# A spectral filter followed by an MLP: eight one-batch units in fixed order, per-row 64-point matrices, a single-pass 49-point stage back, and batch 0's first corner turn on TensorE

## Chip, cores and metric

One core of one Trainium2 chip. The metric is device time in microseconds (us) of one execution. Medians are over the runs of one kernel on one chip; every later kernel was timed together with the kernel before on the same chip (runs 9 to 11 on another chip than runs 1 to 8 and 12, so across these the ratios are what to compare). One of the first three runs of the kernel before took 1411.37 us; it is an outlier.

TensorE is PE in the profile, its weight loads PEld, VectorE DVE, ScalarE ACT, GpSimd POOL, SyncE SP. A suffix q (ACTq, SPq) marks a row in which the engine's sequencer issues something, such as a DMA.

## The reference

```python
X = np.fft.rfft(x, axis=1)                     # x: 8 x 3136 x 256, f32
y = np.fft.irfft(X * (filt_r + 1j * filt_i)[None], n=3136, axis=1)
xt = y.transpose(0, 2, 1)
h = xt @ U @ V                                 # U: 3136 x 32, V: 32 x 3136
u = y + h.transpose(0, 2, 1)
out = u + np.maximum(u @ w_ch1, 0.0) @ w_ch2   # w_ch1: 256 x 1024, w_ch2: 1024 x 256
```

Both kernels factor 3136 as 64 x 49. A batch goes through a 64-point stage, a corner turn through DRAM (store in one layout, load in another: the tiles `asb` out, `a2` in), a 49-point stage, the filter product, a 49-point stage back, a second corner turn (`esb` out, `e2` in), and a last 64-point stage that also adds the low-rank term. Then comes the MLP: eight steps of two hidden-layer matmuls per group of 512 tokens, with the second layer of the group before woven in.

## The kernel before

Five units of 1, 1, 2, 2 and 2 batches. Each middle is a generator; a plan deals its pieces over the MLP steps of earlier units. The parts that matter here:

```python
UNITS = [[0], [1], [2, 3], [4, 5], [6, 7]]
# ... first 64-point stage f1: one matrix wx for all rows, evicted to asb, stored to ct1
pf = ps.tile([128, 2, 512], F32, tag="w", bufs=1, name="pf")
nc.tensor.matmul(pf[:, i, :], wx, u.x[c][:, r:r + 2, :], start=True, stop=True)
# ... the middle: 49-point stage, products with both halves of the filter,
nc.vector.tensor_mul(uv.rearrange("p (f b d) -> p f b d", f=2, b=nb), zin, fin)
# ... and the 49-point stage back: two accumulating passes
for l in range(2):
    nc.tensor.matmul(pe[0:98, 0:bd], g3[:, (2 * k + l) * 98:(2 * k + l + 1) * 98],
                     uv[:, l * bd:(l + 1) * bd], start=(l == 0), stop=(l == 1))
# ... the low-rank term: the spectrum is loaded from DRAM once more, in another layout (eh)
nc.sync.dma_start(eh[c][2 * a:2 * z], dram(u.ct2, ...))
nc.tensor.matmul(ph[32 * g:32 * g + 32, 0:bd], ut2[:, rp * RANK:(rp + 1) * RANK], eh[c][:, i, :],
                 start=(rp < 4), stop=(rp >= 20 and g != 0))
```

Of the kernel before, what the change touches and what calls it, by code (L numbers as in the profile page):

```python
# [12 lines left out]
RELU = mybir.ActivationFunctionType.Relu  # L13

# [5 lines left out]
UNITS = [[0], [1], [2, 3], [4, 5], [6, 7]]  # L20


def _consts():
    f16 = np.float16
    w64 = np.exp(-2j * np.pi * np.outer(np.arange(NQ), np.arange(NQ)) / NQ)
    w49 = np.exp(-2j * np.pi * np.outer(np.arange(NR), np.arange(NR)) / NR)
    tw = np.exp(-2j * np.pi * np.outer(np.arange(NQ), np.arange(NR)) / SEQ)


    wf1 = np.zeros((NQ, 64))  # L30
    wf1[:, 0:31] = w64.real[:, 1:32]
    wf1[:, 31] = w64.real[:, 0]
    wf1[:, 32:63] = w64.imag[:, 1:32]
    wf1[:, 63] = w64.real[:, 32]



    perm = np.arange(NR)
    perm[25:] = 73 - perm[25:]
    tf2 = np.zeros((NK, 98, 98))  # L40
    for a in range(31):
        wp = (w49 * tw[a + 1][None, :])[perm, :]
        tf2[a, 0::2] = np.concatenate([wp.real.T, wp.imag.T], axis=1)
        tf2[a, 1::2] = np.concatenate([-wp.imag.T, wp.real.T], axis=1)
    tf2[:, :, NR + 25:98] *= -1.0
    w0, w32 = w49 * tw[0][None, :], w49 * tw[32][None, :]
    tf2[31, 0::2, 0:25] = w0.real.T[:, 0:25]
    tf2[31, 0::2, NR + 1:NR + 25] = w0.imag.T[:, 1:25]
    tf2[31, 1::2, 25:NR] = w32.real.T[:, 0:24]
    tf2[31, 1::2, NR + 25:98] = w32.imag.T[:, 0:24]  # L50
    tf2[31, 1::2, NR] = w32.real.T[:, 24]
    tf2 = np.concatenate([tf2, tf2[:, :, 0:NR]], axis=2)

    ctw = np.exp(2j * np.pi * np.outer(np.arange(33), np.arange(NR)) / SEQ)
    g = np.zeros((NK, 2, 98, 98))
    for a in range(31):
        t1 = (w49.conj() * ctw[a + 1][:, None]) / SEQ
        tr, ti = t1.real.T[perm, :], t1.imag.T[perm, :]
        g1, g2 = g[a, 0], g[a, 1]
        g1[:NR, :NR], g1[:NR, NR:] = tr, ti  # L60
        g1[NR:, :NR], g1[NR:, NR:] = -tr, -ti
        g2[:NR, :NR], g2[:NR, NR:] = -ti, tr
        g2[NR:, :NR], g2[NR:, NR:] = -ti, tr
        g2[25:NR, :] *= -1.0
        g2[NR + 25:98, :] *= -1.0
    t0 = (w49.conj() * ctw[0][:, None] / SEQ).T
    t32 = (w49.conj() * ctw[32][:, None] / SEQ).T
    g1, g2 = g[31, 0], g[31, 1]
    g1[0, :NR] = t0.real[0]
    g1[NR, NR:] = t32.real[24]  # L70
    g1[1:25, :NR], g1[NR + 1:NR + 25, :NR] = 2 * t0.real[1:25], -2 * t0.real[1:25]
    g2[1:25, :NR], g2[NR + 1:NR + 25, :NR] = -2 * t0.imag[1:25], -2 * t0.imag[1:25]
    g1[25:NR, NR:], g1[NR + 25:98, NR:] = 2 * t32.real[0:24], -2 * t32.real[0:24]
    g2[25:NR, NR:], g2[NR + 25:98, NR:] = -2 * t32.imag[0:24], -2 * t32.imag[0:24]

    w = np.exp(2j * np.pi * np.outer(np.arange(NQ), np.arange(33)) / NQ)
    s2 = np.zeros((64, NQ))
    s2[0:62:2] = 2.0 * w.real[:, 1:32].T
    s2[1:62:2] = -2.0 * w.imag[:, 1:32].T
    s2[62] = w.real[:, 0]  # L80
    s2[63] = w.real[:, 32]

    wf1d = np.zeros((128, 320))
    s2t = np.zeros((64, 320))
    for h in range(2):
        wf1d[h::2, 64 * h:64 * h + 64] = wf1
        wf1d[h::2, 128 + h:256:2] = wf1
        s2t[:, 128 * h + h:128 * h + 128:2] = s2.T
    wf1d[0:64, 256:320] = wf1
    s2t[:, 256:320] = s2.T  # L90

    kr = np.zeros((128, 96))
    for i in range(4):
        kr[32 * i:32 * i + 32, 64:96] = np.eye(32)
    return (wf1d.astype(f16),
            tf2.transpose(1, 0, 2).reshape(98, NK * 147).astype(f16),
            g.transpose(2, 0, 1, 3).reshape(98, NK * 2 * 98).astype(f16),
            s2.astype(f16),
            s2t.astype(f16),
            kr.astype(f16))  # L100


class Unit:
    def __init__(self, n, batches):
        self.n = n
        self.b = batches
        self.nb = len(batches)
        self.bd = self.nb * DM
        self.gt = self.nb
        self.ng = 6 * self.nb  # L110
        self.nr = 8 // self.nb
        self.x = {}
        self.e2 = {}
        self.ready = False
        self.h1 = None
# [3 lines left out]
def kernel(  # L119
# [12 lines left out]
    wf1_np, tf2_np, g_np, s2_np, s2t_np, kr_np = _consts()  # L132

    def inline(a, name):
        return nc.inline_tensor(np.ascontiguousarray(a), name=name).ap()

    wf1_d, tf2_d, g_d = inline(wf1_np, "wf1"), inline(tf2_np, "tf2"), inline(g_np, "g3")
    s2_d, s2t_d, kr_d = inline(s2_np, "s2"), inline(s2t_np, "s2t"), inline(kr_np, "kr")

    units = [Unit(n, b) for n, b in enumerate(UNITS)]  # L140
    for u in units:
        u.ct1 = nc.dram_tensor(f"ct1_{u.n}", (NR, 64, u.bd), F16, kind="Internal")
        u.ct2 = nc.dram_tensor(f"ct2_{u.n}", (32, 98, u.bd), F16, kind="Internal")
# [3 lines left out]
    ps = ctx.enter_context(tc.tile_pool(name="ps", bufs=2, space=bass.MemoryType.PSUM))  # L147
# [3 lines left out]



    def load_x(u, c, after=None):
        st = SEQ * DM if u.nb == 2 else 24 * DM
        if c == 3 * u.nb:
            t = sb.tile([128, DM], F16, tag="xl", bufs=2, name="xl")
            if after is not None:
                hold(t[0:1, 0:1], after)
            src = [[NR * DM, 64], [st, u.nb], [1, DM]] if u.nb == 2 else [[NR * DM, 64], [1, DM]]  # L160
            nc.gpsimd.dma_start(t[0:64 * u.nb],
                                dram(x.tensor, (u.b[0] * SEQ + 48) * DM, src))
        else:
            t = sb.tile([128, 8 * DM], F16, tag="x", bufs=4, name="x")
            if after is not None:
                hold(t[0:1, 0:1], after)
            nc.gpsimd.dma_start(t, dram(x.tensor, (u.b[0] * SEQ + 8 * c) * DM,  # L167
                                        [[NR * DM, 64], [st, 2], [1, 8 * DM]]))
            t = t.rearrange("p (r d) -> p r d", d=DM)
        u.x[c] = t  # L170

    def hold(dst, src):

        nc.vector.tensor_copy(dst, src)

    wf1 = cst.tile([128, 320], F16)
    nc.sync.dma_start(wf1, wf1_d)
    for c in range(4):
        load_x(units[0], c)
    tf2 = cst.tile([98, NK * 147], F16)  # L180
    s2 = cst.tile([64, 64], F16)
    kr = cst.tile([128, 96], F16)
    s2t = cst.tile([64, 320], F16)
    g3 = cst.tile([98, NK * 2 * 98], F16)


    fab = cst.tile([98, 2, NK, DM], F16)

    def load_filters(a, z):

        n = min(z, 31) - a
        for p0, src in ((0, filt_r), (NR, filt_i)):
            nc.gpsimd.dma_start(
                fab[p0:p0 + 25, 0, a:a + n, :],
                dram(src.tensor, (a + 1) * DM, [[64 * DM, 25], [DM, n], [1, DM]]))
            nc.gpsimd.dma_start(
                fab[p0 + 25:p0 + NR, 0, a:a + n, :],
                dram(src.tensor, (63 - a) * DM, [[64 * DM, 24], [-DM, n], [1, DM]]))
        if z == NK:
            for p0, src in ((0, filt_r), (NR, filt_i)):  # L200
                nc.gpsimd.dma_start(fab[p0 + 25:p0 + NR, 0, 31, :],
                                    dram(src.tensor, 32 * DM, [[64 * DM, 24], [1, DM]]))
            nc.gpsimd.dma_start(fab[0:25, 0, 31, :], dram(filt_r.tensor, 0, [[64 * DM, 25], [1, DM]]))
            nc.gpsimd.dma_start(fab[NR + 1:NR + 25, 0, 31, :],
                                dram(filt_i.tensor, 64 * DM, [[64 * DM, 24], [1, DM]]))
            nc.gpsimd.dma_start(fab[NR:NR + 1, 0, 31, :],
                                dram(filt_r.tensor, 1568 * DM, [[DM, 1], [1, DM]]))

    def mirror_filters(a, z):
        nc.sync.dma_start(fab[0:NR, 1, a:z, :], fab[NR:98, 0, a:z, :])  # L210
        nc.sync.dma_start(fab[NR:98, 1, a:z, :], fab[0:NR, 0, a:z, :])

    PARTS = [0, 8, 16, 24, NK]
    KA = PARTS[1] * 98
    load_filters(PARTS[0], PARTS[1])
    usb = sb.tile([64, NR * RANK], F16, tag="och", bufs=2, name="usb")
    vnat = sb.tile([128, SEQ], F16, tag="och", bufs=2, name="vnat")
    w1sb = cst.tile([128, 2 * 1024], F16)
# [7 lines left out]
    def second_loads(src):  # L226
        for i in range(2, 4):
            load_part(i, src)
# [499 lines left out]
```

## Time and profile before

| | before |
|---|---|
| time, median | 632.64 us (630.98 to 1411.37, 3 runs); 630 to 632 in later sets |
| span of the profiled run | 629.3 us, mean granted clock 0.926 |
| busy: PE / DVE / ACT / POOL | 552.8 / 330.0 / 334.6 / 41.7 us |
| DMA | 110.18 MB |

Busy time of PE is not the price of its work, because matmuls overlap in the trace: one of 512 columns is recorded as 0.38 us long, and in a full stretch the next starts 0.22 us after it. The price is the distance from one start to the next, and the prediction works with that. The strip below is from the page of the kernel before. The span is cut in 40 slices of 15.7 us; a digit is the busy share in tenths.

```profile
PE   3294576999699993989999999999999999999997
```

From slice 19 on PE is full, but for the end. Before it, PE is short of data in places.

### The profile page before, as it was taken

Reading aid. Unit: us, or ns where it says so; the run is one execution under the profiler, and the core shown is the slowest. Engines: PE = TensorE matmul, PEld = TensorE weight load, DVE = VectorE, ACT = ScalarE, POOL = GpSimd, SP = SyncE. Lnnn points to the kernel's source line nnn. Section 1 sums busy time; section 2 is a strip of 40 time slices with the busy share of each in tenths; the row PEclk is TensorE's granted clock in tenths of the full one; section 3 lists DMA queues with packets and bytes.
Section 4 is the critical chain, followed back from the end, with each engine's and each line's share of the span. In section 5 each row is a group of like instructions: output and inputs, shape, how many; then the busy total and the mean of one; then the engine's idle time right before and its main releaser. Section 6 shows DMA issues by size and latency. Waiting matters only on the chain.

```text
span 629.3 us, 10769 instructions
## 1 busy us (share of the span) xinstructions
PE 552.8 (88%) x4350; PEld 388.0 (62%) x4350; DVE 330.0 (52%) x390; ACT 334.6 (53%) x623; POOL 41.7 (7%) x62
## 2 busy tenths in 40 slices
PE   3294576999699993989999999999999999999997
PEld 0183242767456661657766676777677767777776
DVE  5274222786278870263888743576866325333332
ACT  0043232667156662546667665665766655666663
POOL 3345110100000000000000000000000000000000
PEclk9558576999979997989999999999999999999999
DMA  9898979999835749868567787455433862331112
GB/s 176 230 205 193 214 183 236 246 250 244 244 119 161 216 81 286 208 166 227 171 187 173 208 245 249 156 148 187 120 131 119 239 202 83 99 100 67 66 67 102
DMA packets 68002, 110.18 MB, mean 175 GB/s; under 512 B 5549, under 2 KB 49438, under 8 KB 66604
## 3 DMA queue, kind: packets, MB, share of 16 engines
q1 hardware_dynamic: 36240, 81.17, 41.2%
q0 software_dynamic: 7312, 15.91, 15.8%
q10 hardware_dynamic: 24400, 12.41, 6.9%
q8 instruction: 34, 0.56, 0.4%
q14 instruction: 16, 0.13, 0.1%
HBM read 72.38 MB, written 51.38 MB: 197 GB/s over the span
## 4 chain that ended last, share of the span: by engine, by line
PE 73%; DMA 16%; issue 4%; DVE 3%; ACT 2%; ACTq 1%; POOL 0%; SPq 0%; POOLq 0%; DVEq 0%
PE phh L550 25%; PE pc L590 24%; PE pe L360 8%; PE pz L382 5%; PE pu L532 3%; PE pc L564 3%; DMA x<-in_x_dram 3%; PE pf L304 3%; DMA ct_3<-asb 2%; DMA g_78<-g 2%; DMA eh<-ct_1 2%; ACTq L320 1%; DMA eh<-ct_2 1%; DMA ct_0<-asb 1%; PE ph L476 1%
## 5 line engine op out<-in xcount | busy, mean ns | idle before, releaser
L550 PE MATMUL phh<-ut,w1sb 128*128 128x512 f16 (+2 forms) x848 | 251.7, 377 | 3.5 <-DVE ut L539 3.0
L397 DVE TENSOR_TENSOR uv<-pz,fab 98x1024 f16<-98x1024 f32 (+1 forms) x128 | 137.8, 1087 | 35.3 <-PE pz L382 34.8
L600 DVE COPY och<-pc 128x512 f32<-128x512 f32 x96 | 66.3, 690 | 165.8 <-PE pc L564 162.6
L550 PEld LDWEIGHTS <-w1sb 128*128 128x128 f16 x848 | 105.6, 146 | 36.7 <-issue 16.7
L366 ACT CAST esb<-pe 98x512 f16<-98x512 f32 (+1 forms) x160 | 79.5, 501 | 64.6 <-PE pe L360 57.0
L360 PE MATMUL pe<-uv,g_78 98*98 98x512 f16 (+1 forms) x320 | 85.7, 353 | 1.4 <-DMA g_78<-g 0.8
L539 DVE CAST ut<-pu 128x1024 f16<-128x1024 f32 (+1 forms) x51 | 59.9, 1174 | 21.6 <-PE pu L532 21.4
L564 PE MATMUL pc<-idn,ut 128*128 128x128 f16 x394 | 54.8, 220 | 0.0
L360 PEld LDWEIGHTS <-g_78 98*98 98x98 f16 x320 | 41.3, 132 | 19.4 <-issue 5.6
L564 PEld LDWEIGHTS <-ut 128*128 128x128 f16 x394 | 38.7, 98 | 6.7 <-issue 0.3
L382 PEld LDWEIGHTS <-tf_74 98*98 98x98 f16 x160 | 21.7, 136 | 20.2 <-DMA a_163<-ct_0 15.3
L304 PE MATMUL pf<-x,wf_64 128*128 128x512 f16 x84 | 27.9, 402 | 6.8 <-DVE ut L539 6.3
L476 PE MATMUL ph<-eh,ut_94 128*32 128x512 f16 (+1 forms) x120 | 10.7, 384 | 26.2 <-DMA eh<-ct_0 11.6
L167 POOL DMA_DIRECT2D x<-in_x_dram x24 | 14.1, 602 | 266.5 <-PE pf L304 225.1
L309 DVE CAST asb<-pf 128x1024 f16<-128x1024 f32 x21 | 25.6, 1219 | 11.5 <-PE pf L304 8.9
L307 ACT CAST asb<-pf 128x1024 f16<-128x1024 f32 x21 | 21.3, 1013 | 10.7 <-PE pf L304 6.7
L390 DVE TENSOR_TENSOR uv<-pz,fab 98x512 f16<-98x512 f32 x32 | 20.9, 687 | 5.1 <-PE pz L387 2.9
L476 PEld LDWEIGHTS <-ut_94 128*32 128x32 f16 x120 | 3.3, 97 | 31.6 <-issue 20.7
L366 ACT ACT_TABLE_LOAD x1 | 1.3, 1283 | 30.2 <-DVE uv L390 30.2
L382 PE MATMUL pz<-a_161,tf_74 98*98 98x256 f16 x8 | 3.2, 403 | 15.2 <-DMA a_163<-ct_0 14.9
L532 PEld LDWEIGHTS <-eb_97 96*128 96x128 f16 x256 | 10.3, 100 | 7.5 <-issue 4.7
L486 ACT CAST hp<-ph 128x512 f16<-128x512 f32 (+1 forms) x5 | 2.5, 501 | 23.1 <-PE ph L483 23.1
(1427 smaller groups left out, 1046.2 us busy)
## 6 DMA issues: line engine op xcount, KB each, us to landing
out_dram<-och SPq DMA_DIRECT2D x48, 512.0 KB
x<-in_x_dram POOLq DMA_DIRECT2D x24, 512.0 KB, 8.0
ct_2<-esb SPq DMA_DIRECT2D x16, 196.0 KB
ct_3<-esb SPq DMA_DIRECT2D x16, 196.0 KB
ct_4<-esb SPq DMA_DIRECT2D x16, 196.0 KB
ct_2<-asb ACTq DMA_DIRECT2D x6, 512.0 KB
ct_3<-asb ACTq DMA_DIRECT2D x6, 512.0 KB
eh<-ct_2 SPq DMA_DIRECT2D x6, 512.0 KB
```

The costliest lines, as they stand in the source:

```text
L304: nc.tensor.matmul(pf[:, i, :], wx, u.x[c][:, r:r + 2, :], start=True, stop=True)
L309: nc.vector.tensor_copy(dst, pf)
L360: nc.tensor.matmul(pe[0:98, 0:bd], g3[:, (2 * k + l) * 98:(2 * k + l + 1) * 98], uv[:, l * bd:(l + 1) * bd], start=(l == 0), stop=(l == 1))
L366: nc.scalar.copy(st["esb"][:, i, :], pe[0:98, 0:bd])
L382: nc.tensor.matmul(pz[0:98, 0:bd], wz, a2[c][:, i, :], start=True, stop=True)
L397: nc.vector.tensor_mul(uv.rearrange("p (f b d) -> p f b d", f=2, b=nb), zin, fin)
L532: nc.tensor.matmul(pu[:, dh, 64 * i:64 * i + 64], e2[0:96, d0:d0 + 128], sv[0:96, 64 * r:64 * r + 64], start=(i == 0), stop=True, skip_gro ...
L539: nc.vector.tensor_copy(gr.ut[:, :, 0:n].rearrange("p h (c q s) -> p h c q s", q=64, s=2), pu[:, :, 0:n].rearrange("p h (c s q) -> p h c q ...
L550: nc.tensor.matmul(ph[:, 0:n], w1v[:, dh, :, t], gr.ut[:, dh, 0:n], start=(dh == 0), stop=(dh == 1))
L564: nc.tensor.matmul(o[:, dh * 128:dh * 128 + 128], gr.ut[:, dh, t0:t0 + n], idn, start=False, stop=(dh == 1), skip_group_check=True)
L590: nc.tensor.matmul(o, gr.h[tt][:, i * 128:(i + 1) * 128], w2sb[:, tt * DM:(tt + 1) * DM], start=(tt == 0), stop=False, skip_group_check=True)
L600: nc.vector.tensor_copy(dst, gr.pc.rearrange("p (j d) -> p j d", j=2))
```

## The change

The intent: give TensorE less work (one pass instead of two in the 49-point stage back; no reload of the spectrum for the low-rank term), and give the scheduler nothing to decide, with one fixed program order of eight equal units, so that the losses of the first half go away. The diff is 1247 lines; its core:

```diff
-UNITS = [[0], [1], [2, 3], [4, 5], [6, 7]]
+NB = 8
+    ctx.enter_context(tc.manual_schedule())
 ...  # 64-point stage: one matrix per row, twiddle inside
-    nc.tensor.matmul(pf[:, i, :], wx, u.x[c][:, r:r + 2, :], start=True, stop=True)
+    nc.tensor.matmul(pf[:, i * DM:(i + 1) * DM], wf[:, 8 * c + 2 * j + i, :], xt[b, c][:, 2 * j + i, :], ...)
 ...  # its result is stored by ACT, as before, from two buffers (three before)
+    asb = sb.tile([128, 8, DM], F16, tag="asb", bufs=2, name="asb")
+    nc.scalar.dma_start(dram(ct1[b], ...), asb[64 * h:64 * h + 64])
 ...  # batch 0: x is the weight, so the result comes out turned; copied to fc, then transposed
+    nc.tensor.matmul(z[:, 128 * i:128 * i + 128], xt[0, c][:, g + i, 128 * hh:128 * hh + 128],
+                     wf[:, 8 * c + g + i, :], ...)
+    dst = free(fc, 0, 128, 3136 * hh + 2 * (24 * h + 8 * c + g), [[2, 4], [1, 2], [98, 32]])
+    src = z.rearrange("p (i h c a) -> p h i c a", h=2, c=2, a=32)[:, h]
+    nc.vector.tensor_copy(dst, src)          # or nc.scalar.copy
 ...  # low rank in the spectrum: U is transformed once (uh), esb is read where it lies
+    nc.gpsimd.tensor_add(uh[:, :, p:p + 8], t[0], t[1])
+    nc.tensor.matmul(ph[32 * g:32 * g + 32, 0:DM], uh[:, a, :], esb[b, a // 4][:, a % 4, :], ...)
 ...  # the complex product: three products on DVE, one sum on POOL, then one pass on PE
+    nc.vector.tensor_mul(ta, pz, va)
+    nc.vector.scalar_tensor_tensor(out=tb[0:64], in0=pz[64:128], scalar=-1.0, in1=vb, op0=MULT, op1=MULT)
+    nc.vector.tensor_mul(tb[64:128], pz[0:64], vb)
+    nc.gpsimd.tensor_add(ys[k], ta, tb)
 ...
+    nc.tensor.matmul(pe[0:98], g3[:, m, :], v, start=(n == 0), stop=(n == len(parts) - 1))
 ...  # order of the start
+    u_hat()
+    for c in range(4):
+        turned(c)
+    mid_first()
+    ...                                      # load_e2, low_rank(0), put_h
+    stage4(groups[0], 0)
+    stage4(groups[0], 1)
+    for _ in st1(1):
+        pass
```

Batch 0 keeps the two passes. All of batch 0's transform and batch 1's first stage now stand ahead of the first hidden-layer matmul; the moment at which that matmul starts is called T0 below.

## The prediction

> **What bounds the kernel now.** I read three views, in this order: the busy table by stretches of time (length, then busy time and instruction count of PE, weight load, DVE, ACT, POOL, then granted clock, DMA share, GB/s), the PE timeline inside the last stretch, and the chain that ended last (start, length, what it was).
>
> ```profile
> 0.00:120.00 120.00, 69.66 (x394) 44.80 (x395) 49.02 (x89) 33.87 (x71) 34.22 (x49) 0.72 0.91 207
> 120.00:300.00 180.00, 158.54 (x1202) 106.84 (x1201) 105.04 (x120) 97.37 (x192) 6.33 (x11) 0.93 0.76 202
> 300.00:620.00 320.00, 319.79 (x2708) 232.07 (x2706) 174.16 (x180) 201.69 (x356) 1.15 (x2) 1.00 0.48 149
> ```
>
> From 300 us on TensorE has no idle time and the full clock; before that it is badly fed.
>
> ```profile
> 560.07 0.63 PE L532 MATMUL pu<-sv,eb_97 96*128 96x64 f16 x16
> 560.54 0.28 PE L590 MATMUL pc<-w2sb,h_6564 128*128 128x256 f16 x1
> 560.65 0.27 PE L590 MATMUL pc<-w2sb,h_6574 128*128 128x256 f16 x1
> ...
> 561.85 0.28 PE L564 MATMUL pc<-idn,ut 128*128 128x128 f16 x2
> 561.96 0.60 PE L550 MATMUL phh<-ut,w1sb 128*128 128x512 f16 x2
> 562.40 0.27 PE L590 MATMUL pc<-w2sb,h_6564 128*128 128x256 f16 x1
> ...
> 261.63 0.40 PE L476 MATMUL ph<-eh,ut_94 128*32 128x512 f16 x4
> 261.96 0.28 PE L590 MATMUL pc<-w2sb,h_2636 128*128 128x256 f16 x1
> ```
>
> Start to start is the real price of a matmul: 0.217 us for 512 columns (0.44 for two), 0.109 for 256, 0.055 for 128, 0.029 for 64 (0.47/16). Four low-rank matmuls with 32 weight columns start within 0.33 us, 0.083 each. Pricing every matmul of the kernel before: hidden layer, second layer, residual and last DFT stage of the 48 full groups 378 us; small groups 8.6; first DFT stage 21.3; the 49-point stage forward 31.3 and back 55.5 (192 x 0.217 + 128 x 0.109); low rank and its 96-row merge 9.4; rest 0.7. Sum 505 us. The matmuls in 300:620 price at about 316 us, so there the prices hold to 1.5%. That leaves 184 us of work in the first 300 us: **116 us are lost there**, and 5 at the end.
>
> ```profile
> 9.72 7.16 DMA ct_0<-asb
> 16.96 6.25 DMA ct_0<-al
> 23.25 4.47 DMA a_161<-ct_0
> 28.58 10.14 DMA g_78<-g
> ...
> 69.42 13.53 DMA x<-in_x_dram
> ...
> 159.70 9.85 DMA eh<-ct_1
> ...
> 230.67 10.60 DMA ct_3<-asb
> 241.27 7.31 DMA eh<-ct_2
> ```
>
> The losses are round trips through DRAM and loads on the path: batch 0's first corner turn (9.7 to 27.7), the tables (28.6), batch 1's x while the MLP already runs (69.4), and the low-rank reload of the spectrum (eh) at 159.7 and 241.3.
>
> **What the Trainium skill says.** (1) "TensorE: Matmul & The Clock Gate", Back-to-back issue gap: N/2.4 + 2.5 ns when warm, 216 ns at 512. The trace agrees (0.43 to 0.44 us for two). (2) The same page, Part 3 on packing: matmuls with few output rows placed in different column groups run together. It agrees, 0.33 us for four. (3) "VectorE: DVE Perf Modes", the perf-mode tier table: tensor_tensor with a PSUM operand runs at 1x. It agrees: 687 ns at 512 elements and 1221 at 1024 is 1.04 ns per element. So a product over 64 partitions should cost what one over 128 does. (4) "GPSIMD Engine Reference", section 3.1: about 2.6 cycles an element for a two-input op, so an estimate of 2.2 us for the new 1024-element adds; no run here shows it yet.
>
> **The change part by part.**
>
> *49-point stage back.* It was two accumulating passes per element; now it is one for batches 1 to 7, because the complex filter product is summed on DVE and POOL first. Batch 0 keeps two. Matmuls: 135 x 0.217 + 18 x 0.109 = 31.2 us instead of 55.5: **-24 us of PE**. Forward stays at 31.2.
>
> *Low rank in the spectrum.* It reads the esb tiles from SBUF, so the reload of eh goes (27 loads, about 12.8 MB) with its waits. 256 x 256 columns: I scale 0.083 by half, 256 x 0.042 = 10.7, plus 0.9: +2 us of PE.
>
> *First stage.* One 64-point matrix per row, so 168 x 256 columns instead of 84 x 512, same columns: 19 us, and 2.8 for batch 0. Transposes for batch 0: 64 x 0.055 = +3.5.
>
> PE sum after: 378 + 8 + 22 + 31 + 31 + 12 + 3.5 + 1 = **486 us against 505**. Only 19 us come from less work; the rest has to come from the 116 us.
>
> *Prologue.* Program order is fixed now, and all of batch 0 and the first stage of batch 1 precede the first MLP matmul. I work out that moment, T0. Loads: 6.2 MB by the software queue; its whole traffic is 15.9 MB at 15.8% of 629 us, or 160 GB/s, so 39 us; some 3.8 MB by hardware queues at about 310 GB/s, 12 us; data is there by about 52 us. Compute: two DVE memsets of 4096 words (4.3 us each, from 0.27 us at 256 words), the 3136-element copy (3.3) and eight products (3.2) end near 16 us; the turned first stage ends near 21; then ACT is the limit of batch 0's middle: 8 copies of 1024 (1.0) + 5 of 1024 (1.0) + 16 of 512 (0.586) = 22.4 us, to about 46. Storing and reloading the second corner turn takes 8 to 9 (store 2.5, load 3, h rows 2.5), to 55; st1(1), 13 evictions and 7 stores issued from ACT, 8 more. **T0 = about 64 us**, close to the loads, with 21 us of priced work done. In the kernel before, the MLP starts at 74 us but only runs freely from 114 and stops again at 160 and 230.
>
> *After T0.* 486 - 21 = 465 us of PE, at the 1.5% of the steady stretch 472. Batch 1's second corner turn has only 5 steps between its stores and its first use while x of batch 2 loads: 8 us. Other stalls: below, 8. End after the last matmul: 5.4 as now. Span 64 + 472 + 8 + 8 + 5 = 557; the time on record is 3.3 us over the span, so **561 us**.
>
> **Do the other engines keep up?** In a middle phase a step (one eighth of a group) costs PE 0.98 for the MLP + 4 x 0.217/4.3 + 0.06 = 1.24 us. DVE: three products of 1.22 per 4.3 steps (0.85) + output copies 0.17 + ut 0.09 = 1.11. ACT: 0.60 + esb 0.27 + asb 0.16 + ut 0.08 = 1.11, plus DMA issues. Both near 89%, against 54 and 63% in the kernel before's last stretch. POOL: 2.2 per 4.3 steps.
>
> **The rivals.** (a) *DVE or ACT becomes the bound in the middle phases.* For: 89%, strict order, one pz pair of banks, one eviction bank. Against: the plan leaves about four steps between the last product and its use, and averages over a batch are 82% (ACT) and 71% (DVE). If half-partition products cost 1.6 us or the POOL add slows DVE, seven phases of 34 steps lose 0.1 to 0.2 us a step, 25 to 45 us: 585 to 605. (b) *The prologue is bound by DMA or the order of waits.* For: DMA share 0.91 in the first 120 us, and ACT-issued stores took 4.1 and 5.2 us per pair at 93.7 and 98.9. Then T0 is 80 or more: 575 to 580. (c) *All waits vanish*: T0 58 and no stalls: 538. (d) *The gain is only the PE work*, because the losses move to other transfers: 632 - 19 = 613. Against: the biggest named waits (eh reloads, g table, batch 0's corner turn) have no counterpart in the new code.
>
> **Range and chances.** Low end (c); high end (a) and a part of (b): 540 to 597. Faster by over 2% needs under 620; even (d) gives that. Faster 0.95, same 0.04, slower 0.01.
>
> **What would show each step.** Right: total PE matmul work falls though the count rises; first hidden-layer matmul between 58 and 72 us; PE over 95% busy from about 80 us on, clock 1.0; ACT between 380 and 420 us busy in all, DVE near 340; POOL adds 2.0 to 2.6 us; no wait on a reload before the low-rank matmuls. Wrong: PE gaps every few steps on pz or y (rival a), T0 past 80 (rival b), stage-back matmuls waiting for POOL, or gaps at unit borders waiting for e2 loads (rival d).

## The result

| | before | after |
|---|---|---|
| time, median | 632.92 us (4 runs) | 624.1 us (621.3 to 626.36, 4 runs) |
| span profiled | 629.3 us | 621.1 us |
| busy PE / DVE / ACT / POOL | 552.8 / 330.0 / 334.6 / 41.7 | 514.4 / 360.9 / 397.6 / 174.0 us |
| matmuls | 4350 | 4467 |
| DMA | 110.18 MB | 95.31 MB |

The ratio is 0.9877, with a 95% interval of 0.983 to 0.9925. Ratios and intervals here are from fast runs timed together, so not quite the ratio of the medians quoted. Executions over 1.5% slower than the fastest of the same kernel are left out of the means. The kernel is 1.2% faster, and 63 us slower than predicted. PE's busy time fell by 38 us, yet the span fell by 8.

The strips of the kernel after (slices of 15.5 us):

```profile
PE   2128545898899889999999889998989889999997
DMA  9971485369656584696548775697364454443212
```

The start is worse fed than before: PE is below 0.6 in slices 1 to 7 but for slice 4, and DMA is not full for much of that time either (slices 3 to 5 and 7). And the long full stretch of the kernel before has become a row of nines and eights: a little is lost everywhere. In the busy table by stretches, cut at T0 (length, then busy time and count of PE, PEld, DVE, ACT, POOL, then clock, DMA share, GB/s):

```profile
0.00:98.00 98.00, 37.95 (x288) 25.77 (x289) 48.40 (x46) 41.62 (x52) 44.54 (x53) 0.89 0.67 137
98.00:621.00 523.00, 476.49 (x4179) 350.48 (x4178) 312.45 (x327) 355.93 (x668) 129.45 (x76) 0.99 0.58 157
```

Against the prediction's price of PE's work, 505 us before and 486 after, the losses are 629.3 - 505 = 124 us before and 621.1 - 486 = 135 us after. So PE's work fell by 19 us and the losses rose by 11: **the waits that the prediction named (the reload of `eh`, the tables, batch 0's first corner turn) did go, and losses of the same size came.** After, 98 - 21 = 77 us are lost ahead of T0 and 523 - 465 = 58 after it.

Not all of this loss is waiting. PE stood idle for 629.3 - 552.8 = 76.5 us before and for 621.1 - 514.4 = 106.7 after; the other 48 and 28 us lie inside its busy time, where it ran slower than the price. The kernel before was busy for 6.73 of the 7 us from 73 to 80, at a granted clock of 0.58. So the idle time grew by 30 us and the slow running shrank by 19, while the mean clock rose from 0.926 to 0.972.

**Ahead of T0.** The timeline of the kernel after at the start, VectorE first (start, length, what; in brackets the idle time before it and what ended it):

```profile
13.28 2.01 DVE L229 TENSOR_TENSOR ut<-psum,tw 98x256 f32<-98x256 f32 x4 [0.96 <-PE psum L224]
28.43 2.00 DVE L229 TENSOR_TENSOR ut<-psum,tw 98x256 f32<-98x256 f32 x4 [13.14 <-POOL uh L233]
30.28 14.74 DVE L294 CAST fc<-psum 128x256 f16<-128x256 f32 x12
```

DVE did half of its eight products by 15.3 us and then stood for 13.14 us, because it needed the buffers that POOL's sum `uh` (L233) reads. The same kernel on GpSimd:

```profile
27.07 0.57 POOL L210 DMA_DIRECT2D w2sb<-in_moe_w_ch_dram  x1
27.63 1.44 POOL L233 TENSOR_TENSOR uh<-ut 98x256 f16<-98x256 f32 x2
```

POOL was not slow: it was issuing the filter's and the weights' loads, which stand ahead of the sum in its program, until 27.6. Then the twelve copies of the turned first stage took DVE 14.74 us. The groups of the two engines' copies:

```profile
L296 ACT CAST fc<-psum 128x256 f16<-128x256 f32 x12 | 14.9, 1687 | 21.0 <-PE psum L278 21.0
L294 DVE CAST fc<-psum 128x256 f16<-128x256 f32 x12 | 14.7, 1593 | 0.0
```

1.59 to 1.69 us each for 256 elements a partition; the prediction's own rate from another row (687 ns for 512) with its slope of 1.04 ns per element would give 0.42. Last, ScalarE just ahead of T0:

```profile
86.81 1.07 ACT L249 CAST asb<-psum 128x512 f16<-128x512 f32 x2 [2.00 <-PE psum L242]
87.91 1.80 ACTq L253 DMA_DIRECT2D ct<-asb  x2
95.04 1.07 ACT L249 CAST asb<-psum 128x512 f16<-128x512 f32 x2 [7.16 <-DMA ct<-asb]
```

ACT waited 7.16 us until a store had freed one of the two `asb` buffers, and PE's first hidden-layer matmul waited in turn for ACT, until T0:

```profile
98.15 2.29 PE L462 MATMUL psum<-ut,w1sb 128*128 128x512 f16 x5 [9.89 <-ACT al L261]
```

**After T0.** What TensorE waited for from 100 to 616 us in the kernel after (total us, times, longest). Its PSUM tiles all go by the name psum; L335 is the 49-point stage, L327 the one back, L394 the low-rank merge, L448 the last 64-point stage, L462 the hidden layer:

```profile
PE psum L462 <- ACT h L465: 9.0, 13, 1.1
PE psum L335 <- DVE tb L596: 8.3, 9, 1.5
PE psum L335 <- DMA a<-ct: 8.0, 7, 2.0
PE psum L327 <- ACT esb L309: 6.4, 4, 1.8
PE psum L394 <- ACT hp L392: 3.3, 7, 0.5
```

With four smaller rows 41.0 us in all, where the kernel before lost almost nothing after 300 us. No wait is longer than 2 us. ACT stands behind half of them, though it is busy only 64% of the time. Its program also holds the issues of the stores; whether these are the cause is tested in run 6.

### The profile page after: what moved, and what is told of

Read it like the earlier page. It is cut to its first block, busy times and chain, and to the rows that moved or that the text cites. A ratio compares the mean times of both kernels' runs of the same rounds, so it can differ in the third digit from the quotient of the medians.

```text
span 621.1 us, 11266 instructions
## 1 busy us (share of the span) xinstructions
PE 514.4 (83%) x4467; PEld 376.3 (61%) x4467; DVE 360.9 (58%) x372; ACT 397.6 (64%) x719; POOL 174.0 (28%) x129
## 2 busy tenths in 40 slices
DMA packets 82597, 95.31 MB, mean 153 GB/s; under 512 B 6853, under 2 KB 63640, under 8 KB 82544
## 3 DMA queue, kind: packets, MB, share of 16 engines
q0 software_dynamic: 7360, 15.91, 15.5%
## 4 chain that ended last, share of the span: by engine, by line
PE 58%; DVE 9%; ACT 8%; DMA 8%; ACTq 4%; issue 4%; SPq 1%; POOL 1%; DVEq 0%; POOLq 0%
PE psum L494 21%; PE psum L462 20%; ACTq L253 4%; PE psum L335 4%; DMA a<-ct 4%; PE psum L327 3%; PE psum L448 3%; ACT asb L249 3%; PE psum L470 3%; ACT h L465 2%; DVE tb L596 2%; DVE tb L593 2%; ACT esb L309 2%; PE psum L242 2%; DMA ct<-asb 1%
## 5 line engine op out<-in xcount | busy, mean ns | idle before, releaser
L465 ACT ACTIVATE h<-psum 128x512 f16<-128x512 f32 (+1 forms) x416 | 238.2, 577 | 136.5 <-PE psum L462 110.8
L462 PE MATMUL psum<-ut,w1sb 128*128 128x512 f16 (+1 forms) x832 | 241.9, 374 | 19.1 <-ACT al L261 9.9
L494 PE MATMUL psum<-w2sb,h 128*128 128x256 f16 x1536 | 232.0, 274 | 0.0
L598 POOL TENSOR_TENSOR y<-ta,tb 128x1024 f16<-128x1024 f16 x56 | 118.9, 2122 | 330.1 <-DVE tb L596 294.8
L494 PEld LDWEIGHTS <-h 128*128 128x128 f16 x1536 | 143.8, 98 | 62.2 <-issue 2.6
L462 PEld LDWEIGHTS <-w1sb 128*128 128x128 f16 x832 | 104.5, 145 | 47.3 <-issue 32.5
L502 DVE COPY och<-psum 128x512 f32<-128x512 f32 x96 | 66.2, 689 | 90.8 <-PE psum L470 90.2
L591 DVE TENSOR_TENSOR ta<-psum,fb 128x1024 f16<-128x1024 f32 x56 | 68.6, 1225 | 41.1 <-PE psum L335 37.8
L309 ACT CAST esb<-psum 98x512 f16<-98x512 f32 x128 | 74.9, 590 | 10.4 <-PE psum L327 7.9
L593 DVE SCALAR_TENSOR_TENSOR tb<-psum,fc 64x1024 f16<-64x1024 f32 x56 | 68.7, 1226 | 1.4
L596 DVE TENSOR_TENSOR tb<-psum,fc 64x1024 f16<-64x1024 f32 x56 | 68.2, 1218 | 1.0
L335 PE MATMUL psum<-a,w2t 98*128 98x512 f16 x135 | 41.5, 386 | 18.5 <-DVE tb L596 8.3
L448 PEld LDWEIGHTS <-e 96*128 96x128 f16 x768 | 36.2, 99 | 33.7 <-issue 16.2
L249 ACT CAST asb<-psum 128x512 f16<-128x512 f32 x78 | 45.6, 587 | 16.4 <-PE psum L242 8.8
L448 PE MATMUL psum<-sv,e 96*128 96x64 f16 x768 | 39.2, 195 | 14.1 <-issue 8.2
L327 PE MATMUL psum<-y,g 128*98 128x512 f16 x105 | 39.8, 379 | 6.9 <-ACT esb L309 6.4
L296 ACT CAST fc<-psum 128x256 f16<-128x256 f32 x12 | 14.9, 1687 | 21.0 <-PE psum L278 21.0
```

The costliest lines, as they stand in the source:

```text
L309: nc.scalar.copy(esb[b, k][:, 2 * half:2 * half + 2, :].rearrange("p s d -> p (s d)"), pe[0:98])
L335: nc.tensor.matmul(pz, w, a, start=True, stop=True)
L448: nc.tensor.matmul(pu[:, 64 * i:64 * i + 64], e2[b, c][:, i, 128 * dh:128 * dh + 128], sv[:, 64 * r:64 * r + 64], start=(i == 0), stop=Tru ...
L462: nc.tensor.matmul(ph[:, 0:n], w1sb[:, dh, :, t], gr.ut[:, dh, 0:n], start=(dh == 0), stop=(dh == 1))
L465: nc.scalar.activation(h[:, 0:n], ph[:, 0:n], RELU)
L494: nc.tensor.matmul(o, gr.h[tt][:, i * 128:(i + 1) * 128], w2sb[:, tt, :], start=(tt == 0), stop=False, skip_group_check=True)
```

## The experiments

The theory: the change's own savings are there, and are covered by (1) POOL's order ahead of `uh`, (2) the scattered copies of the turned stage, (3) the stores that ScalarE issues, and after T0 by (4) the order in which SyncE issues and (5) VectorE's three products in the middles. The rival for each is that the wait is hidden behind another one that lasts as long, so that its removal moves nothing. T0 and the rest of the span are read from the one profiled execution of each, times from all timed ones; kernels are built on each other as told.

| kernel | median us | ratio to before (95%) | T0 | span - T0 |
|---|---|---|---|---|
| after | 624.1 | 0.9877 (0.983-0.9925) | 98.15 | 523 |
| 1 `uh` on DVE | 614.52 | 0.9729 (0.9661-0.9797) | 88.58 | 521 |
| 2 copies' order | 614.91 | 0.9727 (0.9671-0.9783) | 86.53 | 524 |
| 3 three `asb` | 623.71 | 0.9875 (0.9817-0.9932) | 97.04 | 526 |
| 4 = 1 + 2 + 3 | 601.05 | 0.9525 (0.9462-0.9587) | 74.23 | 520 |
| 5 = 4 + early stage | 595.53 | 0.9447 (0.9361-0.9532) | 69.57 | 525 |
| 6 = 4 + SP stores | 587.87 | 0.9304 (0.9245-0.9363) | 67.80 | 523 |
| 7 = 4, two passes back | 620.37 | 0.9817 (0.9764-0.9871) | 75.92 | 543 |
| 8 = 4, no turn on PE | 621.4 | 0.9835 (0.9774-0.9895) | 83.10 | 534 |
| 9 = 4 + early + SP stores | 582.1 | 0.9231 (0.919-0.9272) | 62.94 | 516 |
| 10 = 9 + a2 by POOL | 569.0 | 0.9027 (0.8956-0.9098) | 60.23 | 509 |
| 11 = 10, DVE cut (wrong result) | 567.12 | 0.8986 (0.8944-0.9028) | 65.85 | 500 |
| 12 = 10 + batch 1's a2 by POOL | 569.38 | 0.9004 (0.8961-0.9046) | 61.44 | 506 |

The spread of repeated runs is about 1%, so differences of 2 to 3 us between neighbours of the table mean nothing. T0 has a spread of its own: the wait for batch 0's second corner turn, which lies ahead of it, took from 4.95 to 10.06 us in runs 9 to 12.

### 1. The sum `uh` on VectorE

```diff
-            nc.gpsimd.tensor_add(uh[:, :, p:p + 8], t[0], t[1])
+            nc.vector.tensor_add(uh[:, :, p:p + 8], t[0], t[1])
```

> Theory: in the changed kernel's prologue DVE stands idle from 15.3 to 28.4 us because the four sums of the low-rank factor (POOL, 0.72 us each) queue behind POOL's 19 filter-load issues, which end at 27.6. With the four sums on DVE instead, nothing else touched, the turned first stage runs on, the first hidden-layer matmul comes 10 to 13 us earlier (85 to 88 instead of 98) and the whole time falls by the same, to 611 to 614. Rival: the filters or x are the real limit (the loads on POOL's queue run to about 33 us); then the first product of batch 0 waits for a load, and the time falls by under 4 us.

614.52 us, T0 9.6 us earlier and the median 9.6 us lower. The theory holds, at just under the 10 to 13 us expected. The sum itself costs DVE 0.43 us each, less than it took POOL (0.72), but what counts is that it no longer stands behind twenty-odd load issues.

### 2. The order of the elements in the copies

```diff
-                               [[2, 4], [1, 2], [98, 32]])
-                    src = z.rearrange("p (i h c a) -> p h i c a", h=2, c=2, a=32)[:, h]
+                               [[98, 32], [2, 4], [1, 2]])
+                    src = z.rearrange("p (i h c a) -> p h a i c", h=2, c=2, a=32)[:, h]
```

Same elements, same places; only the order of the walk differs. Before, neighbours in the walk are written 98 elements (196 bytes) apart; now eight of them lie side by side, and the reads from PSUM are the scattered ones (the copy of the last row, L287, is turned likewise).

> Theory: the 24 turned copies take 1.24 us from start to start instead of 0.39 because their innermost run writes 2-byte elements 196 bytes apart. With the loops turned round (8 adjacent elements innermost in the write, strided reads from PSUM instead) each falls to about 0.4 us, the twelve on DVE take 5 us instead of 14.7, and the time falls by about 10 us, to 614. Rival: the cost is the odd access pattern as such, on whichever side it lies; then the copies stay at 1.2 us and the time does not move.

The groups of this kernel, the same two as shown above:

```profile
L294 DVE CAST fc<-psum 128x256 f16<-128x256 f32 x12 | 4.2, 412 | 0.3 <-PE psum L278 0.3
L296 ACT CAST fc<-psum 128x256 f16<-128x256 f32 x12 | 3.7, 384 | 25.1 <-PE psum L278 25.1
```

1593 ns became 412 and 1687 became 384, on both engines; T0 came 11.6 us earlier. The Trainium skill, "Advanced Engine Details and Errata", SBUF Cachelines, says that SBUF has 16-byte lines and that an access to another line each time is penalised. This case agrees and puts a size on it: a factor of about four for 2-byte writes, and none to be seen for the equally scattered PSUM reads. Only runs of one and of eight elements were tried, so which length is enough stays open.

### 3. Three buffers for the first stage's result

```diff
-            asb = sb.tile([128, 8, DM], F16, tag="asb", bufs=2, name="asb")
+            asb = sb.tile([128, 8, DM], F16, tag="asb", bufs=3, name="asb")
```

> Theory: the first stage of batch 1 stops from 88 to 95 us because its third asb tile waits for the store of the first (two buffers, 8.8 us to land). With three buffers the first hidden-layer matmul comes 6 to 7 us earlier (91 instead of 98) and the time falls by 6 us, to 618; in the later batches nothing changes, since there the stores have 12 us. Rival: the stores block the ACT queue anyway or the a2 load, which needs the same stores, then waits as long at step 5; then under 2 us are won.

A miss: 623.71 us, T0 97.04, where 618 and 91 were expected. The wait for the buffer went, and ACT's sequencer was then held by issuing the stores instead (2.52 and 3.03 us for the second and third pair). The rival holds: most of the wait was a mask over the time in which these stores get through. Some of the gain is hidden by spread: the second corner turn ended 2 us later here (82.83 against 80.85), and from there to T0 it took 14.2 us instead of 17.3.

### 4. All three

> All three together. Theory: the prologue is a serial chain and PE is near its limit after it, so the three add: first hidden-layer matmul at 66 to 70 us, time 592 to 597. Rival: a shorter prologue runs into the loads (filters, second-layer weights, x of batch 1) or the pace after the prologue is set by something other than where it starts; then at most half, 608 to 612.

601.05 us. T0 fell by 23.9 us and the rest of the span stayed at 520 (523 in the kernel after): **what is taken from the start passes to the end one for one.** The total was some 4 us short of what was expected (592 to 597), and so was T0 (66 to 70). ScalarE's stores remain: 42 issues of 0.65 us at the median and up to 2.26, and at 250.9 us, for one, ScalarE stood 1.45 us ahead of its next eviction, behind a pair of them.

### 5. Batch 1's first stage ahead of group 0's last stage

```diff
+    for _ in st1(1):
+        pass
     stage4(groups[0], 0)
     stage4(groups[0], 1)
-    for _ in st1(1):
-        pass
```

> The version with all three prologue edits (0.9525 of the kernel before, about 601 us), and the first stage of batch 1 moved ahead of the last stage of group 0 in program order, so that it runs while TensorE waits for the reload of batch 0's second corner turn (idle 50.9 to 60.1 us there). Theory: that wait and the 12 us of batch 1's first stage (62 to 74 us, of which 6.7 are ACT issuing stores) then overlap; first hidden-layer matmul at 62 to 65 us instead of 74, time lower by 9 to 12, ratio about 0.935. Rival: the stores of batch 1 then compete with the reload, and what is won in the overlap is lost there; ratio 0.945 or more.

T0 69.57, not the 62 to 65 expected, and about 5 us of the total. The stage fits into the wait for the second corner turn, but its stores now fall among that turn's transfers. On ScalarE:

```profile
59.08 7.20 ACTq L253 DMA_DIRECT2D ct<-asb  x2
```

Two issues held ACT for 7.20 us. Moving the work early is right only if the stores don't take the engine that also evicts.

### 6. The stores issued by SyncE

```diff
-                nc.scalar.dma_start(dram(ct1[b], (24 * h + 8 * c) * 64 * DM, ...
+                nc.sync.dma_start(dram(ct1[b], (24 * h + 8 * c) * 64 * DM, ...
```

> All three prologue edits, and the first-stage stores (ct1) issued from SP instead of ACT. Theory: each pair of stores holds ACT's instruction stream for 1.2 to 1.5 us (42 issues of 0.65 us each in the median), three pairs a batch, and TensorE then waits for a hidden-layer eviction, a spectrum eviction or a first-stage eviction: some 15 of the 40 us of idle between 80 and 580 us. From SP they cost ACT nothing: waits for ACT fall by half or more, plus 5 us in the prologue; time lower by 10 to 15 us, ratio about 0.933. Rival: SP runs its issues in order, so a store that waits for its eviction holds up the a2 and e2 loads behind it; the waits on a2 grow by as much, ratio 0.95.

587.87 us, 13 us less than the kernel it is built on. From 85 to 580 us TensorE's waits for ScalarE fall from 21.6 us in run 4 to 6.3, and those for `a2` grow: 15.6 us, against 7.1 in run 4, and 9.07 more at 80.7. TensorE's waits from 80 to 585 us:

```profile
PE psum L335 <- DMA a<-ct: 24.7, 7, 9.1
...
PE psum L327 <- ACT esb L309: 0.9, 3, 0.3
PE psum L462 <- ACT h L465: 0.8, 1, 0.8
```

Both the theory and a part of the rival hold. SyncE is in order as well, as its timeline at the border near 203 us shows:

```profile
196.14 0.32 SPq L312 DMA_DIRECT2D ct<-esb  x1
202.32 0.47 SPq L408 DMA_DIRECT2D e<-ct  x1
202.84 0.59 SPq L408 DMA_DIRECT2D e2l<-ct  x1
203.53 0.51 SPq L303 DMA_DIRECT2D a<-ct  x1
```

The load of `e2` waited until 202.32 for the store of `esb`, and the load of the next batch's `a2`, which needed nothing from it, waited behind it. TensorE then stood 4.38 us for that `a2`, and paid for it twice. Its clock, the third number from the end, was full before the wait and half after it:

```profile
200.00:203.00 3.00, 3.00 (x29) 2.16 (x28) 0.69 (x1) 2.21 (x5) 0.00 (x0) 1.00 0.27 70
207.00:213.00 6.00, 5.59 (x26) 3.04 (x26) 2.47 (x3) 1.19 (x2) 0.00 (x0) 0.50 1.01 277
```

By these numbers the slow 5.59 us cost an estimated 2.8 more. In the profiled executions the rest of the span is 523 us, no less than run 4's 520: the whole gain that they show is T0's 6.4 us. By the medians some 7 of the 13 us come after T0; the profiled execution of run 6 was its slowest (592.39).

### 7. The 49-point stage back twice

Built on 4. The inverse matmuls of batches 1 to 7 run twice; the second run overwrites the first with the same values, so the result is correct.

```diff
-            stage3(pe, [(ys[k][:, 512 * half:512 * half + 512], 0, 1)], (k, half) == (7, 1))
+            for _ in range(2):
+                stage3(pe, [(ys[k][:, 512 * half:512 * half + 512], 0, 1)], (k, half) == (7, 1))
```

> All three prologue edits, and every inverse 49-point matmul of batches 1 to 7 run twice (same result): 105 x 0.217 + 14 x 0.109 = 24 us of TensorE put back, the amount that the single pass is to save. Theory: TensorE is the bound between 80 and 590 us (92% busy, its waits single events), so the time rises by 20 to 24 us; ratio about 0.99. Rival: the pace of the middle phases is set by DVE and ACT (near 89% by my sum), and the added matmuls fall into waits that are there anyway; then it rises by under 12 us, ratio under 0.972.

620.37 us, 19 more (20 to 24 expected), for 24 us of matmuls added. So TensorE is the bound for about four fifths of the time in which these run, and the single pass is worth about 19 us, close to its full price.

### 8. Batch 0's first corner turn through DRAM again

Built on 4. The diff is abridged: batch 1's `x` is then loaded from within `st1(0)`, and VectorE takes half of batch 0's evictions there.

```diff
-    for c in range(4):
-        turned(c)
+    for _ in st1(0):
+        pass
-            ...                              # eight transposes and one copy per a2 tile
+            a2[k] = load_a2(0, k)
```

> All three prologue edits, but batch 0's first corner turn through DRAM again, as in the kernel before: first stage, store, reload, in place of the turned matmuls and the transposes. Theory: the trip costs 12 to 13 us after the last eviction (15.3 to 27.9 us in the kernel before), the turned way with quick copies 5 us of copies and no trip; first hidden-layer matmul 8 to 10 us later (82 to 84), time higher by the same, ratio about 0.967. Rival: the transposes and their copies of 1.0 us each in the ACT-bound middle of batch 0 cost as much as the trip; then within 3 us, ratio 0.95 to 0.957.

621.4 us, 20 more than with the turn, twice what was expected, though T0 came 8.9 us later, within the 8 to 10 expected. TensorE's timeline:

```profile
41.13 1.87 PE L335 MATMUL psum<-a,w2t 98*128 98x512 f16 x4 [17.30 <-DMA a<-ct]
```

The trip through DRAM held TensorE for 17.30 us and ran from 24 to 41. TensorE's hidden layer then starts at 83.10 and runs freely only from 91. So the turn on TensorE is worth some 20 us, in a kernel whose copies and whose POOL order are mended. The part itself was sound; its copies and the sum ahead of it, which cost 23.9 us together with the third buffer (run 4), took more than that.

### 9. Early stage and SyncE's stores together

> The three repairs, the early batch-1 first stage and the stores issued by SyncE, together. The early move alone left T0 at 69.57 because the third store pair held ScalarE 7.2 us; the SyncE stores alone left T0 at 67.80 with one wait of 9.07 us for the first batch-1 a2 at 80.7. Theory: with SyncE issuing, ScalarE is free for the copies of batch 1's first stage, and the stores are done well before that a2 is fetched, so T0 falls to 62 to 66 and the 9.07 us wait is gone; total 587.87 - 9 - 2 to 5 = 573 to 578 us. Rival (SyncE's own order: the early stores stand behind the e2 loads and esb stores of batch 0 or ahead of them and delay them): T0 stays at 68 or more and the total at 583 or more.

582.1 us, 19 less than run 4, with T0 at 62.94 in the range expected. It was run on another chip. The total is 4 us above the range. The 9.07 us wait of run 6 shrank to 5.5; the rest of it was not the stores' lateness alone.

### 10. The a2 loads issued by GpSimd

```diff
-        nc.sync.dma_start(t, dram(ct1[b], 4 * k * DM, [[NK * DM, 98], [1, 4 * DM]]))
+        eng = nc.sync if b == 1 else nc.gpsimd
+        eng.dma_start(t, dram(ct1[b], 4 * k * DM, [[NK * DM, 98], [1, 4 * DM]]))
```

> As the run with the early first stage and SyncE's stores, and the a2 loads of batches 2 to 7 are issued by GpSimd instead of SyncE. With SyncE's stores, TensorE lost 15.6 us in six waits for a2 at the borders between batches, each behind loads of e2 that were themselves waiting in SyncE's order for the esb store. Theory (head of line in SyncE's order): the six waits fall to 3 us or less in sum and the total falls by 9 to 13 us against the run beside it. Rival 1 (the transfer itself is late, because the DMA engines are full there or the stores land late): waits stay at 10 us or more, total within 4 us of the run beside it. Rival 2 (GpSimd's adds hold the loads back): waits for a2 appear within the middles, not only at the borders.

569.0 us, 13 less than the run beside it. TensorE's waits from 60 us on in run 9, then in run 10 (its lines are one lower):

```profile
PE psum L335 <- DMA a<-ct: 18.4, 7, 5.5
PE psum L448 <- DMA e<-h: 9.3, 2, 7.4
```

```profile
PE psum L449 <- DMA e<-h: 9.6, 5, 2.9
PE psum L336 <- DMA a<-ct: 7.3, 4, 5.1
```

The waits for `a2` fell from 18.4 us in seven to 7.3 in four, of which 5.1 is batch 1's first one (still SyncE's), so the borders lose 2.2. Head of line it was, not the transfer. The Trainium skill, "Perfetto Trace Analysis", DMA Optimizations, says that it may make sense to issue inputs from one engine and outputs from another. This case agrees in part: the 48 loads moved are inputs and gained 13 us, but SyncE kept the loads of `e2` beside its stores. In the table by stretches of run 10, to be read against that of the kernel after:

```profile
0.00:60.00 60.00, 34.87 (x284) 24.11 (x285) 37.50 (x48) 29.51 (x51) 41.79 (x49) 0.98 0.92 184
60.00:569.00 509.00, 473.30 (x4187) 349.07 (x4184) 313.57 (x329) 356.62 (x668) 154.57 (x124) 0.98 0.59 166
```

The start does the same work in 60 us instead of 98, and DMA is now 92% busy in it, where it was 67%: little room is left there. POOL has 25 us more of issues, and no wait of TensorE is put down to it. The largest waits left are those for the rows of `h` (L449), 9.6 us in five.

### 11. One of VectorE's three products taken out

Its output is wrong, which doesn't matter for the time.

```diff
-                nc.vector.scalar_tensor_tensor(out=tb[0:64], in0=pz[64:128], scalar=-1.0, in1=vb,
-                                               op0=MULT, op1=MULT)
+                nc.vector.memset(tb[0:64], 0.0)
```

> As the run with GpSimd's a2 loads, and the scalar_tensor_tensor of each middle step (1.226 us, 56 of them) is replaced by a memset of the same half tile: wrong result on purpose. It takes about 0.9 us of VectorE from each of 56 steps. Theory (the middle's single PSUM pair is freed by VectorE's third product, and VectorE's three products are too slow at the end of a middle): the waits of TensorE for tb, 6.7 to 8.3 us in all runs so far, vanish and the total falls by 5 to 8 us. Rival (those waits are not the binding ones, another takes their place): total within 3 us of the run beside it.

567.12 us, 1.9 less than the run beside it, which by the total alone speaks for the rival. TensorE's waits of this run from 60 us on:

```profile
PE psum L449 <- DMA e<-h: 17.9, 5, 10.1
...
PE psum L336 <- DVE tb L596: 1.8, 6, 0.4
```

The waits for `tb` did fall, from 6.8 to 1.8, and the span after T0 from 509 to 500 us. But T0 of this execution was 65.85, behind a wait of 10.06 us for the second corner turn, which took 4.95 in run 10, 7.45 in run 9 and 7.00 in run 12 with the same instructions there. A part of the 9 us after T0 is only that later start: batch 1's `a2` then cost a wait of 2.47 us instead of 5.11. So the products' wait is real, and an estimate of its worth is the 5 us by which it fell; that the total doesn't show them is put down to the spread of that DMA wait, which these runs don't settle.

### 12. Batch 1's a2 by GpSimd too

```diff
-        eng = nc.sync if b == 1 else nc.gpsimd
+        eng = nc.gpsimd
```

> As the run with GpSimd's a2 loads, now for batch 1 too, whose first a2 SyncE could issue only after six stores (at 72.31 us; TensorE then waited 5.11 us for it at 74.73). Theory: GpSimd issues it as soon as the last store of batch 1's first stage has landed, 2 to 4 us earlier; the wait shrinks to 1 to 3 us and the total falls by 2 to 4 us, to a ratio of 0.896 to 0.900. Rival (the stores themselves are late, so the load has to wait for them on either engine): no change, ratio 0.902 to 0.906. It is also the candidate for the best version of the study, so it is timed with five rounds.

569.38 us, ratio 0.9004 (five rounds); the range reaches from the theory's values to the rival's, so neither is shown. TensorE waited 5.74 us for that `a2`, as long as before. The best version is run 10 or 12, which these rounds don't tell apart: both correct, 9.7 to 10% faster than the kernel before and about 9% faster than the change as made.

## Why the prediction was wrong, by its own steps

**T0 was the larger error: 64 predicted, 98.15 measured.** Its steps, as the prediction put them:

| step | predicted end (length) | measured end (length) | cause |
|---|---|---|---|
| memsets, copy, eight products | 16 | 30.4 | POOL's order, +14 |
| turned first stage | 21 (5) | 45.6 (15) | scattered writes, +10 |
| batch 0's middle | 46 (25) | 71.2 (26) | as predicted |
| second corner turn | 55 (8 to 9) | 80.9 (10) | as predicted |
| group 0's last stage, batch 1's first | 64 (8) | 98.2 (17) | stores from ACT, +9 |

The first step failed because the engines' work was added up by size, and not by place in the program: the POOL sum was seen as cheap, and it is, but it stands behind all of the load issues. The second failed because a copy of 256 elements was priced by count alone, without its access pattern. The last failed because issuing was taken as free beside the evictions; the prediction had even quoted pairs of stores that took 4.1 and 5.2 us in the kernel before, as evidence for its rival (b), and did not carry it into the sum. Runs 1 and 2 recover the first two by 9.6 and 11.6 us, as single edits; the last took runs 5, 6 and 9 (74.23 to 62.94). With all mended T0 is 60 to 66, where the prediction had put it, but that is partly luck: in the order that the prediction reasoned about, with the stores on SyncE, T0 is 67.80 (run 6), and the rest comes from the early stage, which the change doesn't have.

**The stalls after T0 were mis-sized: 16 us predicted (8 for batch 1, 8 for the rest), 41.0 measured.** The prediction compared mean loads of the engines (89% at most) and gave strict order little weight. By run 6 about 15 us of the 41 were ScalarE held by store issues, though its mean load is 64%. Run 10 shows that the `a2` waits that took their place there were SyncE's order; the 8.0 us of `a2` waits in the kernel after itself were not tested apart. Run 11 shows that the `tb` waits are VectorE's products. 523 - 41 - 4.8 (from the last matmul to the end) leaves 477 us against the 472 predicted for the work itself, so that term was 1% off. Two smaller readings were off as well. All of the 116 us lost in the first 300 us before was put down to round trips and loads, though PE was idle there for only 72 of them and ran at a granted clock of 0.72 and 0.93. And the 3.3 us from span to time set a median against the span of another execution; the profiled execution of the kernel after took 622.91 us, 1.8 over its span.

**Rivals.** (b) was right about T0 past 80 and in part about why: it named the order of waits and the stores issued from ACT. Its other ground, DMA share, was not the cause (0.67 ahead of T0). (a) is right in size only: half-partition products took 1.22 us, as predicted, and from 105 to 505 us DVE is 60 to 70% busy and ACT 67 to 71%, so neither is the bound; yet TensorE's waits for the two, 8.3 and 22.9 us, lie in the 25 to 45 us that (a) gave. In total the result lies nearest to (d), 613, and beyond it; but its ground, a move of the losses to other transfers, is only partly it: most of what came was order of issue and the copies, and its sign, waits at unit borders for `e2`, is a single one of 1.8 us.

**What was right.** Matmuls rose in count and fell in busy time. PE was to be over 95% busy at clock 1.0 from 80 us on; from T0 it was 91%, at 0.99. The sum on POOL was estimated at 2.2 us and took 2.12:

```profile
L598 POOL TENSOR_TENSOR y<-ta,tb 128x1024 f16<-128x1024 f16 x56 | 118.9, 2122 | 330.1 <-DVE tb L596 294.8
```

The low-rank matmuls no longer wait for a reload, batch 0's 32 of them take 1.06 us in all. ACT was to be 380 to 420 us busy and was 397.6. DVE was to be near 340 and was 360.9; the scattered copies are 10.5 of the difference (14.7 to 4.2 in run 2). And the 24 us of the single pass were worth about 19, in run 4's kernel (run 7).

## What to carry to other kernels

Each engine took its program in order (runs 1, 6 and 10): before adding a small operation to an engine, look at what stands ahead of it there, and before giving an engine DMA issues, look at what waits behind them. A saving on the bounding engine shows only if the other engines' orders let it: here 19 us less work on TensorE, by the prediction's prices, became 8 us less time, and after six edits of a few lines, none of which touched the arithmetic, 63. For a copy that turns data, walk so that the writes to SBUF are the adjacent ones and let the reads from PSUM be scattered (1.6 to 0.4 us a copy in run 2).

## What the Trainium skill lacked or had wrong

- "Advanced Engine Details and Errata", SBUF Cachelines, names the penalty without a size and doesn't say whether it holds for writes by DVE and ACT. The runs: 256 f16 elements per partition, each written 196 bytes from the last, took 1.59 us on DVE and 1.69 on ACT, against 0.41 and 0.38 with runs of 16 bytes.
- The same page, PSUM Cachelines, is about matmuls; for reads by DVE and ACT at 32 and more f32 apart, run 2 shows no such cost (0.38 to 0.41 us for 256 elements).
- "Perfetto Trace Analysis", DMA Instruction — HWDGE, says that the sequencer is held while descriptors are made, but not for how long when the DMA engines are full. Here ACT's store issues took 0.65 us each at the median (run 4), and 7.20 us for a pair at 59 us of run 5, where the DMA share was 1.07.
- No page read gives the cost of a cheap operation that stands behind load issues on GpSimd: here 13.14 us of VectorE's time, for a 0.72 us sum.
